# One operand of the next unit prepared ahead of another in a hand-written list of side work (attention, router and two feed-forward layers on one core)

## The chip, the cores and the metric

The kernel runs on one core of a Trainium2 chip. The metric is device time in microseconds: the median over several runs of one launch. Engines are named as in the profile: PE multiplies matrices (PEld loads its weights), DVE, ACT and POOL work elementwise, SP issues the transfers (DMA) between the chip's buffers and DRAM.

## The reference, cut to what matters

```python
x = attention(q, k, v)                       # windowed, 2304 tokens x 512
logits = x @ w_gate;  P = exp(logits - logits.max())
for _ in range(8):                           # the router's normalisation
    P /= P.sum(1, keepdims=True) + 1e-09
    P /= P.sum(0, keepdims=True) + 1e-09
    P *= N / E
out = 0
for e in range(8):                           # D = 512, F = 1024
    out += P[:, e:e + 1] * (np.maximum(x @ w1[e], 0.0) @ w2[e])
h = out @ w_in;  return (h * np.cos(h)) @ w_out      # F = 2048
```

## The kernel before

All products are in float32 written as sums of a high part and a low remainder: an operand x is kept as hi = x rounded (ACT writes it) and lo = x - hi (DVE or POOL writes it), and a product is hi*hi, hi*lo and lo*hi.

After the attention, the experts' layer runs over three blocks of 768 tokens, and inside a block over 32 *units* of 256 columns of F (4 units for each of 8 experts; `UPE` is 4, `NU1` is 32). A unit n is seven products of its first weight matrix with sums of quarters of x (a seven-product scheme), called by number in the order 5, 1, 4 of the unit before, 2, 3, 6, then the *batch*, then 7. The batch multiplies the hidden values of unit n-1 with its second weight matrix, in 6 tiles of 128 tokens (tt = 0 to 5), each into one of three banks `gT` in turn, which DVE then adds to the accumulator (the eviction, L1181 or, once the router's weights are in, L1191).

In the first block, ("moe", 0), the weights are not yet in the form the products need. It is made as side work, unit by unit, by generators: each `yield` ends a step, and the steps are called at fixed places among the products. The four that matter here:

- `prep_s(u)`: POOL makes four sums of quarters of the first matrix of unit u, tile `s` (L133).
- `prep_a(u)`: three ACT copies (hi, L143) and three DVE subtractions (lo, L146; the last one, of 128x1024, from `s`) fill `waX`, the first operand of unit u; then SP stores it to DRAM (`wd`, 1792 KB, L148) and loads the raw first matrix of unit u+2 (`ra`, two transfers, L105). Eight steps.
- `prep_b(u)`: ACT (hi, L160) and POOL (lo, L162) fill `wbX`, the second weight matrix of unit u; three stores of it (`wdp`, 256 KB each, L167). Six steps.
- `prep_sb(u)`: POOL makes four sums of quarters of the second matrix (L182), ACT their hi (L185), DVE their lo (L189), all in one tile `sb` that every unit uses in turn; SP stores hi and lo (`wdp`, 1024 KB, L192) and loads the raw second matrix of unit u+2 (`rb`, L105). These rows are used by later blocks only.

`prep_a`, `prep_b` and `prep_s` stand in the list `pre`, of which only the first entry is stepped; `prep_sb` stands in the list `sbq`. `slot()` steps `pre`, then `sbq`, then (by way of `feed`) `bg`, which holds the router's normalisation: a step A (three small DVE instructions, L410 to L412) and, three steps on, a step B (a matmul with `ones` on PE, L420, and three DVE instructions). There is a slot after products 5, 1, 4, 2 and 7 and after tiles 1 to 5 of the batch, and after each of those tiles `pre` is stepped once more. At the end of a unit the rest of `pre` is run down.

In unit n, `pre` begins with `prep_b(n)`, two steps of which run in the slots after products 5 and 1. Then, at product 4, `begin(n + 1)` adds `prep_a(n + 1)` and `prep_s(n + 2)`.

In units 2 to 4 `prep_sb(n)` has ten steps, one for each slot: ACT's L185 in the slot after product 4, DVE's L189 after tile 1 of the batch, the store and the load of `rb` after tile 3. From unit 5 on it has fewer steps, and L185 falls in the slot after product 5.

Every engine, SP among them, takes its instructions strictly in the order of the program; the framework puts in the waits for data and for buffers.

Of the kernel before, what the change touches and what calls it, by code (L numbers as in the profile page):

```python
# [29 lines left out]
def tile_attention_moe_cos_ffn(ctx, tc, q, k, v, w_gate, w1, w2, w_in, w_out, out):  # L30
# [8 lines left out]
    UPE = F // FU  # L39
# [33 lines left out]
    with tc.manual_schedule():  # L73
# [16 lines left out]
        def load_raw(u, ab):  # L90
            if u >= NU1 + NU2 or (u, ab) in raw_t:
                return
            t = rawp.tile([P, KC, FU] if ab == "a" else [P, 2, DM], F32, tag=f"r{ab}", name=f"r{ab}{u}")
            raw_t[u, ab] = t
            if u >= NU1:
                for c in range(2):
                    nc.sync.dma_start(out=t.rearrange("p k f -> p (k f)")[:, c * 512:(c + 1) * 512],
                                      in_=w32[4 * (u - NU1) + (0 if ab == "a" else 2) + c])
                return
            e, s = divmod(u, UPE)  # L100
            src = (w1[e][:, s * FU:(s + 1) * FU].rearrange("(k p) f -> p k f", p=P) if ab == "a"
                   else w2[e][s * FU:(s + 1) * FU, :].rearrange("(k p) d -> p k d", p=P))
            m = t.shape[1] // 2
            for c in range(2):
                nc.sync.dma_start(out=t[:, c * m:(c + 1) * m, :], in_=src[:, c * m:(c + 1) * m, :])  # L105
# [3 lines left out]
        def wa_of(u):  # L109
            return waX[:, u % 2].rearrange("p (o h k f) -> p o h k f", o=7, h=2, k=2)  # L110
# [15 lines left out]
        def prep_s(u):  # L126
            ra = raw_t[u, "a"]
            s4 = s_t[u] = rawp.tile([P, 4, 2, P], F32, tag="s4", bufs=1, name=f"s4_{u}")
            a11, a12 = ra[:, 0:2, :P], ra[:, 2:4, :P]
            a21, a22 = ra[:, 0:2, P:], ra[:, 2:4, P:]  # L130
            for o, x, y, op in ((0, a21, a22, ALU.add), (1, s4[:, 0], a11, ALU.subtract),
                                (2, a11, a21, ALU.subtract), (3, a12, s4[:, 1], ALU.subtract)):
                nc.gpsimd.tensor_tensor(out=s4[:, o], in0=x, in1=y, op=op)  # L133
                yield

        def prep_a(u):
            ra, s4 = raw_t[u, "a"], s_t[u]
            wa = wa_of(u)
            both = ra[:, :, :P].rearrange("p (o k) f -> p o k f", k=2)
            parts = [(wa[:, 0:2, 0], wa[:, 0:2, 1], both), (wa[:, 2, 0], wa[:, 2, 1], ra[:, 2:4, P:]),  # L140
                     (wa[:, 3:7, 0], wa[:, 3:7, 1], s4)]
            for hi, lo, x in parts:
                nc.scalar.activation(out=hi, in_=x, func=AF.Copy)  # L143
                yield
            for hi, lo, x in parts:
                nc.vector.tensor_tensor(out=lo, in0=x, in1=hi.bitcast(F32), op=ALU.subtract)  # L146
                yield
            nc.sync.dma_start(out=wd1[u], in_=waX[:, u % 2].bitcast(F32))  # L148
            if u + 2 < NU1:
                load_raw(u + 2, "a")  # L150
            yield
# [715 lines left out]
        bg, bg2, pre, feed, sbq = [], [], [], [], []  # L867
# [361 lines left out]
        def begin(n):  # L1229
            if n < len(steps):  # L1230
                kind, b, u = steps[n]
                if kind == "moe" and not b and u >= 2:
                    pre.append(prep_a(u))
            if n + 1 < len(steps):
                kind, b, u = steps[n + 1]
                if not b and kind == "moe" and u >= 3:
                    pre.append(prep_s(u))
# [52 lines left out]
        for n, s in enumerate(steps):  # L1290
            kind, b, u = s
# [20 lines left out]
            for m in (5, 1, 4, 2, 3, 6, 0, 7):  # L1312
# [12 lines left out]
                if m == 4:  # L1325
                    if n:
                        product(steps[n - 1], 4)
                    begin(n + 1)
                else:
                    product(s, m)  # L1330
# [75 lines left out]
```

## Time and profile before

| what | us |
|---|---|
| median of 3 runs | 1981.72 (1981.71 to 1982.1) |
| the profiled execution, whole | 1982.96 |
| its span (first to last instruction) | 1981.2 |
| PE busy | 1957.6 |
| DVE busy | 1555.7 |
| ACT busy | 862.6 |
| POOL busy | 964.7 |

The busy times are sums over the whole span, and the span is some 1.8 us shorter than the execution. Times in a trace count from the start of the span. Unit 2 of the first block begins at about 182 us, unit 3 at 198.6, unit 4 at 216.2 and unit 5 at 233.6.

### The profile page before, as it was taken

To read this page: it belongs to the slowest core of one execution; us is meant where nothing else is said; L and a number is where in the kernel's file an instruction comes from. 1 tells how busy PE (TensorE), PEld (TensorE's weight loads), DVE (VectorE), ACT (ScalarE), POOL (GpSimd) and SP (SyncE) were. 2 spreads that over 40 slices of the span, in tenths; PEclk is the share of its full clock that TensorE was granted. 3 is DMA by queue.
4 is the path that set the end of the run, shared out by engine and by line. 5 is a ranking of instruction groups with operands and counts; after the bars stand their busy time and mean duration, and the time that the engine had idled before them with its cause. 6 is when DMAs were issued, how large, how long until landed. Compare 5 with 4: busy or idle time off the path is not lost.

```text
span 1981.2 us, 31148 instructions
## 1 busy us (share of the span) xinstructions
PE 1957.6 (99%) x10977; PEld 1823.6 (92%) x10977; DVE 1555.7 (79%) x2655; ACT 862.6 (44%) x1617; POOL 964.7 (49%) x940
## 2 busy tenths in 40 slices
PE   8999999999999999999999999999999999999999
PEld 6668899999999999999999999999999999998898
DVE  7885777777777788988888877888877776757766
ACT  6885444444444333333333433333233354554543
POOL 5673566666666445454536622545454423333221
PEclk9999999999999999999999999999999999999999
DMA  7854888888888999998999888999998765554552
GB/s 194 221 141 146 294 294 312 302 310 311 295 309 302 321 333 314 339 336 320 340 326 326 277 285 280 328 337 334 330 306 297 242 223 195 197 218 175 207 192 96
DMA packets 293755, 540.05 MB, mean 273 GB/s; under 512 B 80256, under 2 KB 141792, under 8 KB 286432
## 3 DMA queue, kind: packets, MB, share of 16 engines
q1 hardware_dynamic: 292240, 537.74, 78.7%
q8 instruction: 87, 1.43, 0.3%
q14 instruction: 68, 0.56, 0.1%
q10 hardware_dynamic: 1360, 0.33, 0.1%
HBM read 384.32 MB, written 153.67 MB: 272 GB/s over the span
## 4 chain that ended last, share of the span: by engine, by line
PE 94%; DVE 2%; DMA 2%; ACT 1%; issue 1%; SPq 0%; POOL 0%; DVEq 0%; POOLq 0%; ACTq 0%
PE gT L1111 23%; PE y_moe L972 19%; PE z_moe L972 10%; PE gT L1201 7%; PE gT L1202 7%; PE gT L1200 7%; PE y_ffn L972 5%; PE x_moe L972 5%; PE z_ffn L972 2%; PE xbank L639 2%; DMA wbX<-wdp 1%; PE x_ffn L972 1%; PE s L537 1%; PE pt L603 1%; PE pt L601 1%
## 5 line engine op out<-in xcount | busy, mean ns | idle before, releaser
L1111 PE MATMUL gT<-hX,wbX 128*128 128x384 f32 x2688 | 538.7, 335 | 2.8 <-DMA wbX<-wdp 2.7
L1111 PEld LDWEIGHTS gT<-hX,wbX 128*128 128x128 f32 x2688 | 471.6, 188 | 5.5 <-DMA wbX<-wdp 2.1
L972 PE MATMUL y_moe<-xtT_moe,waX 128*128 128x384 f32 x1728 | 347.3, 335 | 0.0
L972 PEld LDWEIGHTS y_moe<-xtT_moe,waX 128*128 128x128 f32 x1728 | 304.4, 188 | 3.3 <-ACT s_moe L1001 0.6
L1123 DVE TENSOR_TENSOR acc_moe<-gT,acc_moe 128x384 f32<-128x384 f32 x432 | 237.7, 550 | 77.9 <-PE gT L1111 76.0
L1202 PE MATMUL gT<-wbX,hX 128*128 128x512 f32 x660 | 258.2, 391 | 0.0
L1201 PE MATMUL gT<-wbX,hX 128*128 128x512 f32 x660 | 258.1, 391 | 0.0
L1200 PE MATMUL gT<-wbX,hX 128*128 128x512 f32 x660 | 258.0, 391 | 0.0
L1001 ACT ACTIVATE s_moe<-y_moe 128x384 f32<-128x384 f32 x192 | 93.3, 486 | 350.5 <-PE y_moe L972 350.2
L1145 POOL TENSOR_TENSOR hodd<-hodd 128x384 f32<-128x384 f32 x128 | 156.0, 1238 | 139.2 <-DVE hX L1131 71.3
L1145 POOL TENSOR_TENSOR cX<-cX 128x384 f32<-128x384 f32 x128 | 145.7, 1158 | 157.3 <-DVE hX L1131 97.1
L961 POOL TENSOR_TENSOR hX<-cX,hX 128x768 fp32r<-128x768 f32 x44 | 83.5, 1913 | 249.3 <-ACT hX L958 208.6
L133 POOL TENSOR_TENSOR s<-ra 128x256 f32<-128x256 f32 x80 | 59.6, 745 | 236.5 <-DVE waX L146 164.0
L1191 DVE SCALAR_TENSOR_TENSOR acc_moe<-gT,prob,acc_moe 128x512 f32<-128x512 f32 x174 | 129.6, 747 | 37.5 <-PE gT L1202 35.7
L1202 PEld LDWEIGHTS gT<-wbX,hX 128*128 128x128 f32 x660 | 123.9, 188 | 25.9
L1200 PEld LDWEIGHTS gT<-wbX,hX 128*128 128x128 f32 x660 | 124.1, 188 | 25.5 <-DVE acc_moe L1191 0.7
L1201 PEld LDWEIGHTS gT<-wbX,hX 128*128 128x128 f32 x660 | 124.0, 188 | 24.3
L917 ACT ACTIVATE hX<-cX 128x768 fp32r<-128x768 f32 x64 | 43.9, 687 | 216.1 <-DVE cX L1004 216.1
L1131 DVE TENSOR_TENSOR hX<-cX,hX 128x768 fp32r<-128x768 f32 x112 | 131.4, 1173 | 1.6 <-ACT hX L1135 1.6
L1131 DVE TENSOR_TENSOR hX<-hodd,hX 128x768 fp32r<-128x768 f32 x112 | 127.4, 1137 | 0.9 <-ACT hX L1135 0.9
L972 PE MATMUL z_moe<-xtT_moe,waX 128*128 128x384 f32 x576 | 116.6, 336 | 2.6 <-DVE waX L146 2.6
L972 PE MATMUL z_moe<-xtB_moe,waX 128*128 128x384 f32 x576 | 116.1, 336 | 0.0
(211 smaller groups left out, 3768.3 us busy)
## 6 DMA issues: line engine op xcount, KB each, us to landing
waX<-wd SPq DMA_DIRECT2D x264, 512.0 KB, 5.5
wbX<-wdp SPq DMA_DIRECT2D x224, 512.0 KB, 6.6
wd<-waX SPq DMA_DIRECT2D x32, 1792.0 KB, 6.8
wdp<-sb SPq DMA_DIRECT2D x32, 1024.0 KB, 5.8
wdp<-wbX SPq DMA_DIRECT2D x96, 256.0 KB, 4.3
wbX<-wd SPq DMA_DIRECT2D x24, 1024.0 KB, 4.9
waX<-wd SPq DMA_DIRECT2D x88, 256.0 KB, 5.2
ra<-in_moe_w_dram SPq DMA_DIRECT2D x64, 256.0 KB, 7.3
```

The costliest lines, as they stand in the source:

```text
L133: nc.gpsimd.tensor_tensor(out=s4[:, o], in0=x, in1=y, op=op)
L961: eng.tensor_tensor(out=h[:, 1], in0=c, in1=h[:, 0].bitcast(F32), op=ALU.subtract)
L972: nc.tensor.matmul(ps[:, :HB], wa[:, WI[m], wl, kc, :], x[:, xl, kc, :], start=start and kc == 0 and n_ == 0, stop=stop and kc == 1 and n_ ...
L1001: nc.scalar.activation(out=t["s", i], in_=ps[:, :HB], func=AF.Copy)
L1111: nc.tensor.matmul(ps[:, :HB], w[:, u, wl, d * P:(d + 1) * P], x[:, xl, u, :], start=m in (1, 5, 2) and n_ == 0, stop=m in (4, 3, 2) and n ...
L1123: nc.vector.tensor_tensor(out=a, in0=ps[:, :HB], in1=a, op=ALU.add)
L1131: nc.vector.tensor_tensor(out=x[:, 1], in0=H[:, q], in1=x[:, 0].bitcast(F32), op=ALU.subtract)
L1145: nc.gpsimd.tensor_tensor(out=H[:, t[0], c], in0=H[:, t[1], c], in1=H[:, t[2], c], op=ALU.subtract)
L1191: nc.vector.scalar_tensor_tensor(out=a, in0=ps, scalar=pe, in1=a, op0=ALU.mult, op1=ALU.add)
L1200: nc.tensor.matmul(ps, hf[f][:, 0, ts], wb[:, f, 0, :], start=f == 0, stop=False)
L1201: nc.tensor.matmul(ps, hf[f][:, 0, ts], wb[:, f, 1, :], start=False, stop=False)
L1202: nc.tensor.matmul(ps, hf[f][:, 1, ts], wb[:, f, 0, :], start=False, stop=f == 1)
```

## The change

For units u of 2 to 5, `prep_a(u)` is put at the front of `pre` rather than at its end. `UPE + 1` is 5. For u = 2 `pre` is empty at that point, so the order differs for u = 3, 4 and 5, that is inside units 2, 3 and 4, in which two steps of `prep_b` have run already and four are left.

```diff
                 kind, b, u = steps[n]
                 if kind == "moe" and not b and u >= 2:
-                    pre.append(prep_a(u))
+                    pre.insert(0 if u <= UPE + 1 else len(pre), prep_a(u))
             if n + 1 < len(steps):
                 kind, b, u = steps[n + 1]
```

Where the steps fall in units 2, 3 and 4 (a1 to a3 are ACT's copies, a4 to a6 DVE's subtractions, a7 the store of `wd` and the load of `ra`; b3 is POOL's subtraction, b5 the three stores):

| place | before | after |
|---|---|---|
| after product 4 | b3 | a1 |
| after product 2 | b4 | a2 |
| after tile 1 | b5, b6 | a3, a4 |
| after tile 2 | a1, a2 | a5, a6 |
| after tile 3 | a3, a4 | a7, a8 |
| after tile 4 | a5, a6 | b3, b4 |
| after tile 5 | a7, a8 | b5, b6 |

b4, b6 and a8 issue nothing.

## Rows read from the trace of the kernel before

**Rows 1.** The page, busy time: engine, us, share of span, instructions.

```profile
PE 1957.6 (99%) x10977; PEld 1823.6 (92%) x10977; DVE 1555.7 (79%) x2655; ACT 862.6 (44%) x1617; POOL 964.7 (49%) x940
```

**Rows 2.** PE's waits, 195 to 260 us: who for whom, us, times, longest.

```profile
PE z_moe L972 <- DVE waX L146: 2.6, 3, 1.0
```

**Rows 3.** Timeline of PE: start, us, what [idle before <- releaser].

```profile
200.08 0.97 PE L972 MATMUL z_moe<-xtT_moe,waX 128*128 128x384 f32 x4 [1.00 <-DVE waX L146]
200.89 0.42 PE L420 MATMUL gT<-prob,ones 128*128 128x152 f32 x2
...
217.72 0.97 PE L972 MATMUL z_moe<-xtT_moe,waX 128*128 128x384 f32 x4 [1.00 <-DVE waX L146]
...
234.73 0.97 PE L972 MATMUL z_moe<-xtT_moe,waX 128*128 128x384 f32 x4 [0.64 <-DVE waX L146]
```

**Rows 4.** Timeline of DVE, in the batches of units 3 and 4.

```profile
208.81 0.68 DVE L1181 TENSOR_TENSOR acc_moe<-gT,acc_moe 128x512 f32<-128x512 f32 x1
...
212.01 1.28 DVE L1181 TENSOR_TENSOR acc_moe<-gT,acc_moe 128x512 f32<-128x512 f32 x2
...
214.03 0.68 DVE L146 TENSOR_TENSOR waX<-ra,waX 128x512 fp32r<-128x512 f32 x1
...
215.23 0.41 DVE L146 TENSOR_TENSOR waX<-ra,waX 128x256 fp32r<-128x256 f32 x1
...
216.45 1.22 DVE L146 TENSOR_TENSOR waX<-s,waX 128x1024 fp32r<-128x1024 f32 x1
217.59 0.68 DVE L1181 TENSOR_TENSOR acc_moe<-gT,acc_moe 128x512 f32<-128x512 f32 x1
...
230.22 1.41 DVE L1191 SCALAR_TENSOR_TENSOR acc_moe<-gT,prob,acc_moe 128x512 f32<-128x512 f32 x2
```

**Rows 5.** Timeline of SP in unit 3: issues of transfers.

```profile
212.15 0.36 SPq L192 DMA_DIRECT2D wdp<-sb  x1
...
217.70 0.33 SPq L148 DMA_DIRECT2D wd<-waX  x1
218.07 1.43 SPq L105 DMA_DIRECT2D ra<-in_moe_w_dram  x2
```

**Rows 6.** DMA issues: KB each, us to landing; then stores of `sb`, 150 to 260.

```profile
wd<-waX SPq DMA_DIRECT2D x1, 1792.0 KB, 6.7
...
ra<-in_moe_w_dram SPq DMA_DIRECT2D x1, 256.0 KB, 7.3
...
DMA to landing us min/median/max: 4.9/4.9/7.1
```

**Rows 7.** Timeline of ACT in units 3, 4 and 5.

```profile
205.38 1.06 ACT L185 ACTIVATE sb<-sb 128x1024 fp32r<-128x1024 f32 x1 [1.09 <-POOL sb L182]
206.92 0.49 ACT L1001 ACTIVATE s_moe<-y_moe 128x384 f32<-128x384 f32 x1 [0.49 <-PE y_moe L972]
...
223.08 1.06 ACT L185 ACTIVATE sb<-sb 128x1024 fp32r<-128x1024 f32 x1 [1.14 <-POOL sb L182]
...
236.97 1.07 ACT L185 ACTIVATE sb<-sb 128x1024 fp32r<-128x1024 f32 x1 [0.23 <-POOL sb L182]
```

**Rows 8.** Timeline of PE: tiles 3 and 5 of batches; product 6 of unit 5.

```profile
210.78 0.39 PE L1200 MATMUL gT<-wbX,hX 128*128 128x512 f32 x1
...
213.79 0.39 PE L1200 MATMUL gT<-wbX,hX 128*128 128x512 f32 x1
...
231.02 0.50 PE L1200 MATMUL gT<-wbX,hX 128*128 128x512 f32 x1
...
239.69 1.20 PE L972 MATMUL y_moe<-xtT_moe,waX 128*128 128x384 f32 x6
```

**Rows 9.** Stretches of PE: us, busy (instructions), granted clock, DMA share, GB/s.

```profile
18.00:20.00 2.00, 1.25 (x8) 0.80 0.99 308
20.00:22.00 2.00, 2.00 (x8) 0.50 1.11 323
22.00:24.00 2.00, 2.00 (x15) 0.85 1.12 345
```

## The prediction, made before the changed kernel was run

> **What bounds the kernel now.** I read the page first: PE is busy for nearly the whole span [rows 1], so a change outside PE pays only where it removes a wait of PE, and costs where it adds one. Next the list of PE's waits over the stretch that the change touches: there is one entry, product 5 (`z_moe`) waiting three times for the lo parts of `waX` [rows 2]. The timeline of PE places them at the starts of units 3, 4 and 5: 1.00, 1.00 and 0.64 us [rows 3]. Each is the first product that reads what `prep_a` made in the unit before. Then I followed the other engines through one unit, in the order in which the moved steps reach them: DVE, SP, the transfers, ACT. Units 2 and 3 repeat each other at a distance of 17.64 us (200.08 and 217.72 [rows 3]), so unit 3 serves for both.
>
> **What the change can give.** DVE's last subtraction a6 begins at 216.45 and lasts 1.22 [rows 4]: 217.67, and PE goes on at 217.72. After the change a4 to a6 stand around the eviction of tile 2, from 212.01 on. Consecutive DVE instructions overlap by 0.08 (216.45 + 1.22 against 217.59), so a4 0.68, one eviction 0.68, a5 0.41 and a6 1.22 less 3 x 0.08 end at 214.76: 2.9 us earlier, ahead of PE's need. All three waits go, 2.64 us; no more than that can be won.
>
> It isn't all won. DVE's work only changes order, and in the batches of units 2 and 3 it is nearly gapless. The normalisation's step A now comes behind a6, and ends where the last eviction began, 217.59 (+0.08); PE's matmul L420 needs it. In unit 2's place that is 200.03 against L420's start at 200.89 [rows 3]: 0.8 us won rather than 1.00. In unit 4 step A is absent, but the eviction of tile 2 has no room: it ends at 230.22 + 0.75 = 230.97 and tile 5, which takes the same bank, begins at 231.02 [rows 8]; a4 ahead of it delays tile 5 by 0.6, which nearly eats the 0.64. In unit 3 the same bank has room (213.79 against 213.29).
>
> **What it moves on SP.** a7 now stands in the slot after tile 3, and `slot()` steps `pre` before `sbq`: so the store of `wd` and both loads of `ra` come ahead of the store of `sb` on SP, where before the store of `sb` was issued at 212.15 and a7 at 217.70 [rows 5]. The store of `wd` must wait for a6 and SP takes its instructions in order. For t, the end of a6: `wd` is issued at t, the second `ra` at about t + 1.1, `sb` at t + 1.9 (0.33 and 1.43 of issuing with the gaps between).
>
> Landing: the second `ra` needs 7.3 us [rows 6], so t + 8.4. The `sb` store of 1024 KB behind it needs its bytes moved: `wd` with 768 KB more takes 6.7 against 4.9, 1.8 us, so 1024 KB take 2.4. I take t + 10.8. Bounds: if it need not queue, t + 1.9 + 4.9 = t + 6.8; if it only starts when `ra` has landed, t + 8.4 + 4.9 = t + 13.3. The longest landing of an `sb` store in this stretch is 7.1 rather than 4.9 [rows 6], with a store of `wd` and loads before it in the queue; a wait behind earlier bytes is thus real, and I stay near the queueing value.
>
> The Trainium skill, DMA: Bandwidth & Descriptors, section on the anatomy of one DMA, fits a transfer (of the other issuing path) as 2.0 us plus bytes over 436 GB/s. As an estimate by that page, `wd`, two `ra` and `sb` together, 3.4 MB, land in 9.8 us, and the sum below would be 3 us smaller; the rows' durations are a little longer than the fit (6.7 against 6.2 for `wd`), and I use the rows.
>
> **Who waits for it.** `sb` is a single tile. ACT's L185 of the next unit overwrites what the store reads, so it waits for the landing. Before, the store landed at 212.15 + 4.9 = 217.05 and L185 came at 223.08 [rows 7]: 6 us of room. Behind L185 on ACT stand a2 and the copy of product 6 (L1001); DVE's add, step A, all evictions and a4 to a6 follow that copy. So each late landing makes the next a6 late, and that the next landing: one chain through three units.
>
> Unit 2: a6 ends at 214.76 - 17.64 = 197.1; `sb` lands at 207.9.
> Unit 3: L185 at 207.9, not 205.38. It takes 1.06, a2 some 0.4 (under the 0.49 of a wider copy), so L1001 at 209.3, not 206.92: +2.4. The eviction of tile 0 ends at 208.81 + 0.68 + 2.4 = 211.9; tile 3, PE at 210.78, waits for it: +1.2. The eviction of tile 2 ends at 212.01 + 0.68 + 0.6 (a4) + 2.4 = 215.7; tile 5, at 213.79, comes at 215.75: +2.0. Step A ends at 217.67 + 2.4 = 220.1, and L420 (200.89 + 17.64 = 218.53) is at +1.6. a6 ends at 217.1.
> Unit 4: `sb` lands at 227.9; L185 at +4.8, the copy behind it at +5.0. The eviction of tile 2 ends at 230.97 + 5.0 + 0.6 = 236.6; tile 5 at +5.6; at product 5 the old wait of 0.64 is gone, so PE is at +5.0. a6 ends 1.5 after that eviction (0.41 + 1.22 less overlaps), 238.0.
> Unit 5: `sb` lands at 248.8. Here L185 stands already behind product 5, before at 236.97, so it is 11.8 us late. Behind it is the copy of product 1 (L1001): 248.8 + 1.07 + 0.49 less 0.1 of overlap = 250.26. PE's product 6 adds into the bank which that copy reads. Before it ran at 239.69; now at 250.3: **+10.6 us**, of which 5.6 are one empty stretch of PE (ready at 244.7). From there the old order holds, and nothing in it is late again: the next `sb` store has no `wd` ahead of it.
>
> **The clock.** The trace has one fall of PE's clock inside the run, at the end of a stretch in which PE had been waiting (busy 1.25 of 2.00 us): the granted clock is 0.80, 0.50 and 0.85 in three stretches of 2 us, that is at the lower of its levels, 1.2 instead of 2.4 GHz, for part of them [rows 9]. What it cost is 2 x (0.20 + 0.50 + 0.15) = 1.7 us of work. 5.6 us without work is emptier than what stood before this one. I take one such fall, +1.7; bounds 0 and two falls, 3.4.
>
> **What costs nothing.** b3 changes place in the program, but not among POOL's own instructions: between the last sum of one `prep_sb` and the first of the next POOL has nothing else. `wbX` is read a unit later. The loads of `rb` and the stores b5 land later, behind `sb`, by some 10 us; what they bring is read a unit or more on, so they are covered by a whole unit of PE (17.64 us). POOL's sums `s` can start 2.9 us earlier, which nobody waits for.
>
> **Sum.** +10.6 + 1.7 = +12.3, on the profiled execution's 1982.96: 1995.3. That execution is 1.24 above the median shown, so in the runs' scale 1994.0. A landing 1 us shorter or longer is worth three, since three stores stand in the chain.
>
> **The rivals.**
> (a) *The store of `sb` doesn't queue*: it lands at t + 6.8. Then L185 of unit 3 and 4 isn't late, PE is 1.6 ahead, a6 of unit 4 ends at 231.4 and `sb` lands at 238.2; L185 of unit 5 is still 1.25 late, and product 6 starts at 239.7, as before. Time 1981.8: no change. For it: 16 engines share the transfers, and 4.9 is the usual landing. Against: 7.1 when something is ahead. A landing of about 8.6 is where the loss reaches 4 us (10.6 less 3 x 2.2).
> (b) *L185 never waits* (the store's reads are over long before its landing counts, or its bytes overtake): only the gains stay, 1.9 to 2.6 us, 1979.1 to 1979.8, faster but within 0.2%. It decides if L185 in unit 5 still starts by 237. Against it: the tile is single, and the store reads just what L185 writes.
> (c) *Partial queueing*, bytes of both stores interleaved, landing about t + 9: +5.2, perhaps a fall of the clock: 1987 to 1989.
> (d) *Longer landing*, t + 12 to 13.3, with two falls of the clock: +14 + 3.4 to +18 + 3.4: 1999 to 2003.
>
> **Chances.** Forecast 0.62 (1990 to 1998); (a) 0.10; (b) 0.07; (c) 0.12; (d) 0.09. A measurement of this kernel can tell about 0.2%, 4 us, from no change. Forecast, (c) and (d) hold 0.83, of which 0.01 falls short of those 4 us: slower 0.82. (a) and (b) hold 0.17 and stay within 0.2%, since the three waits are 2.64 us in all; I take 0.02 of it for a gain that I haven't seen: faster 0.02, same 0.15 + 0.01 = 0.16. The range holds the forecast and (c) and the lower end of (d): 1986 to 1999.
>
> **What the changed profile would show.** Right: the wait of `z_moe` on `waX` gone; on SP L192 right behind L148 and L105 in units 2 to 4; L185 waiting for the DMA `wdp<-sb` some 4, 5 and more us; PE waiting for evictions in two batches and, longest of all, in unit 5 for ACT's copy `s_moe`; perhaps 0.50 of clock near 250. Wrong: landings of `sb` near 5 us, or L185 at its old places; then (a) or (b) holds. A PE wait for `waX` that stays would mean that the steps are not where I put them.

## The result and the profile after

| | before | after |
|---|---|---|
| median, us (6 runs of each on one chip) | 1983.11 (1981.71 to 1985.42) | 1997.03 (1996.43 to 1998.85) |
| ratio, 95% interval | 1 | 1.0073 [1.0062, 1.0083] |
| span of the profiled execution | 1981.2 | 1995.2 |
| PE busy | 1957.6 | 1963.2 |

The changed kernel is 13.9 us slower; the spans differ by 14.0. Line numbers are the same in both. Up to unit 2 the new trace runs 0.27 us ahead (product 7 of unit 1, the last ahead of unit 2, starts at 180.87, before at 181.14), so 0.27 is added wherever a start of after is compared with one of before. The starts of the other kernels are put on the scale of before by the same product.

First the list of PE's waits over the whole span of the kernel after (who for whom, us, times, longest), cut to the lines that are new and one that shrank:

```profile
PE y_moe L972 <- ACT s_moe L1001: 7.7, 1, 7.7
...
PE gT L1200 <- DVE acc_moe L1191: 2.6, 1, 2.6
PE gT L1200 <- DVE acc_moe L1181: 2.5, 1, 2.5
...
PE gT L1111 <- DMA wbX<-wdp: 1.3, 2, 1.0
...
PE gT L420 <- DVE prob L412: 0.3, 1, 0.3
```

The wait for `waX` [rows 2] is gone, as the change intends. In its place stand 13.1 us of others. The last of them, 0.3 us, is that of L420 for step A, which now comes behind a6. The other 12.8 follow from one wait that PE never shows, ACT's, in the timeline of ACT of the kernel after (start, us, what, idle before and its releaser):

```profile
208.56 1.06 ACT L185 ACTIVATE sb<-sb 128x1024 fp32r<-128x1024 f32 x1 [4.57 <-DMA wdp<-sb]
...
228.51 1.06 ACT L185 ACTIVATE sb<-sb 128x1024 fp32r<-128x1024 f32 x1 [3.73 <-DMA wdp<-sb]
...
251.38 1.06 ACT L185 ACTIVATE sb<-sb 128x1024 fp32r<-128x1024 f32 x1 [9.48 <-DMA wdp<-sb]
252.34 0.47 ACT L1001 ACTIVATE s_moe<-y_moe 128x384 f32<-128x384 f32 x1
```

Before, L185 waited for POOL's sums, 0.2 to 1.1 us [rows 7]; now it waits for the store out of the single tile `sb`. The timeline of SP of the kernel after shows why the store is late:

```profile
196.87 0.34 SPq L148 DMA_DIRECT2D wd<-waX  x1
197.31 1.39 SPq L105 DMA_DIRECT2D ra<-in_moe_w_dram  x2
198.75 1.29 SPq L192 DMA_DIRECT2D wdp<-sb  x1
200.15 3.40 SPq L105 DMA_DIRECT2D rb<-in_moe_w_dram  x2
...
217.67 0.33 SPq L148 DMA_DIRECT2D wd<-waX  x1
...
219.54 1.31 SPq L192 DMA_DIRECT2D wdp<-sb  x1
...
238.57 0.33 SPq L148 DMA_DIRECT2D wd<-waX  x1
...
240.44 1.30 SPq L192 DMA_DIRECT2D wdp<-sb  x1
```

In unit 3 the store of `sb` had gone out 5.6 us ahead of that of `wd` [rows 5]; now it goes out 1.9 us behind it. L185 starts the moment it has landed, so the landing counted from the issue of `wd` is 208.56 - 196.87 = 11.7, 228.51 - 217.67 = 10.8 and 251.38 - 238.57 = 12.8 us. From its own issue a store of `sb` now takes up to 10.8, before at most 7.1 [rows 6]; here the view of the tile `sb`, 180 to 275 us, after:

```profile
DMA to landing us min/median/max: 4.0/8.9/10.8
```

The timeline of PE of the kernel after, at the marks that answer to [rows 3] and [rows 8]:

```profile
199.81 0.53 PE L420 MATMUL gT<-prob,ones 128*128 128x152 f32 x2 [0.30 <-DVE prob L412]
...
212.43 0.79 PE L1200 MATMUL gT<-wbX,hX 128*128 128x512 f32 x1 [2.49 <-DVE acc_moe L1181]
...
220.61 0.53 PE L420 MATMUL gT<-prob,ones 128*128 128x152 f32 x2
...
233.17 0.79 PE L1200 MATMUL gT<-wbX,hX 128*128 128x512 f32 x1 [2.58 <-DVE acc_moe L1191]
...
252.86 2.29 PE L972 MATMUL y_moe<-xtT_moe,waX 128*128 128x384 f32 x6 [7.70 <-ACT s_moe L1001]
...
263.91 1.23 PE L972 MATMUL y_moe<-xtT_moe,waX 128*128 128x384 f32 x6
```

The loss grows along the chain. L420 in unit 2's place is 0.8 us early (199.81 + 0.27 against 200.89), a unit later 2.4 late (220.61 + 0.27 against 218.53), product 6 of unit 5 is 13.4 late (252.86 + 0.27 against 239.69). Product 7, the last of unit 5, is 15.2 late (263.91 + 0.27), by this row of before:

```profile
248.94 1.23 PE L972 MATMUL y_moe<-xtT_moe,waX 128*128 128x384 f32 x6
```

The end of the span is 14.3 late on the same scale: about 1 us comes back later, where the wait of L1111 for `wbX` is 1.3 instead of 2.7.

The clock, in stretches of 2 us of PE of the kernel after (columns as in [rows 9]):

```profile
212.00:214.00 2.00, 1.57 (x4) 0.54 0.04 8
214.00:216.00 2.00, 2.00 (x8) 0.60 0.00 0
...
232.00:234.00 2.00, 0.83 (x2) 0.66 0.00 0
234.00:236.00 2.00, 2.00 (x6) 0.50 0.00 0
236.00:238.00 2.00, 2.00 (x10) 0.98 0.00 0
250.00:252.00 2.00, 0.00 (x0) 0.50 1.09 381
252.00:254.00 2.00, 1.14 (x4) 0.50 0.20 68
254.00:256.00 2.00, 2.00 (x7) 0.50 0.74 287
256.00:258.00 2.00, 2.00 (x9) 0.86 0.96 273
```

After each of the three long waits PE works at the lower level, 1.2 GHz, for some 3 to 4 us. What that costs is read from the time up to the same later product, without the wait. From tile 3 to product 7 it takes 5.94 us behind the first wait (212.43 to 218.37) and 5.56 behind the second (233.17 to 238.73), before 4.37 (210.78 to 215.15) and 4.34 (228.17 to 232.51). From product 6 to product 7 of unit 5 it takes 11.05 (252.86 to 263.91), before 9.25 (239.69 to 248.94). That is 1.6, 1.2 and 1.8, together 4.6 of the 5.6 us by which PE's busy time grew.

### The profile page after: what moved, and what is told of

Its sections match the earlier page's. It is cut to its first block, busy times and chain, and to the rows that moved or that the text cites. A ratio compares the mean times of both kernels' runs of the same rounds, so it can differ in the third digit from the quotient of the medians.

```text
span 1995.2 us, 31146 instructions
## 1 busy us (share of the span) xinstructions
PE 1963.2 (98%) x10977; PEld 1827.0 (92%) x10977; DVE 1555.5 (78%) x2655; ACT 861.9 (43%) x1617; POOL 965.2 (48%) x940
## 4 chain that ended last, share of the span: by engine, by line
PE 92%; DMA 3%; DVE 2%; ACT 1%; issue 1%; SPq 0%; POOL 0%; ACTq 0%; POOLq 0%; DVEq 0%
PE gT L1111 23%; PE y_moe L972 19%; PE z_moe L972 9%; PE gT L1201 7%; PE gT L1200 7%; PE gT L1202 7%; PE y_ffn L972 5%; PE x_moe L972 5%; PE z_ffn L972 2%; PE xbank L639 2%; PE x_ffn L972 1%; PE s L537 1%; DMA wbX<-wdp 1%; DMA wdp<-sb 1%; DMA waX<-wd 1%
## 5 line engine op out<-in xcount | busy, mean ns | idle before, releaser
L1111 PE MATMUL gT<-hX,wbX 128*128 128x384 f32 x2688 | 538.3, 334 | 1.7 <-DMA wbX<-wdp 1.3
L1111 PEld LDWEIGHTS gT<-hX,wbX 128*128 128x128 f32 x2688 | 471.7, 188 | 4.6 <-DMA wbX<-wdp 1.8
```

The source lines that it names most:

```text
L1111: nc.tensor.matmul(ps[:, :HB], w[:, u, wl, d * P:(d + 1) * P], x[:, xl, u, :], start=m in (1, 5, 2) and n_ == 0, stop=m in (4, 3, 2) and n ...
```

## The experiments

Ratios are to the kernel before on the same chip, in runs of the same batch: 1983.26 us (median of 21) for the first four, 1982.37 (21) for the others. Where an edit shifts lines, the profile's numbers shift by some.

**1. The new order on ACT, DVE and POOL, the old order on SP.** The issues of `prep_a` are held until `prep_sb` has issued its own:

```diff
+def out_a():
     nc.sync.dma_start(out=wd1[u], in_=waX[:, u % 2].bitcast(F32))
     if u + 2 < NU1:
         load_raw(u + 2, "a")
+if 3 <= u <= UPE + 1:
+    held.append(out_a)
+else:
+    out_a()
...
 # prep_sb, behind its store and the load of rb
+while held:
+    held.pop(0)()
```

> The changed kernel, with one thing put back: on SP the store of sb and the loads of rb come again ahead of the store of wd and the loads of ra in units 2 to 4; the order on ACT, DVE and POOL stays as changed. Theory (a chain through the single tile sb: L185 waits for the landing of a store that stands behind wd and ra on SP): the wait of L185 on the DMA is gone (0 us), the three waits of PE for waX too, so the time is 1.9 to 2.6 us below the kernel before, some 16 us below the changed one. Rival 1 (the new order on DVE and ACT itself costs, since a4 to a6 stand ahead of evictions that PE waits for): at least some 5 us of the loss stay, PE still waits 2 us or more for evictions. Rival 2 (transfers crowded into the last third of the unit): they are as crowded as before, so most of the loss stays.

Measured: 1980.73 us (1979.57 to 1983.44), ratio 0.9986 [0.9977, 0.9995]. The list of PE's waits, 180 to 300 us, of this kernel has two lines:

```profile
PE gT L429 <- DVE prob L421: 0.6, 2, 0.3
PE gT L1209 <- DVE acc_moe L1200: 0.5, 1, 0.5
```

and its ACT (L192 is L185 of the others) never waits for the DMA in units 3 to 5:

```profile
204.23 1.07 ACT L192 ACTIVATE sb<-sb 128x1024 fp32r<-128x1024 f32 x1
...
234.99 1.05 ACT L192 ACTIVATE sb<-sb 128x1024 fp32r<-128x1024 f32 x1
```

So the whole loss lies in the order of issues on SP, and the rest of the change is a small gain: 2.5 us, by the interval 1.0 to 4.6. Of it 1.5 us are PE's waits in this stretch (2.64 before, 1.1 now); in the trace product 7 of unit 5 comes 1.7 us earlier than before (247.30 less 0.10, against 248.94). What lies beyond that is within the interval. This version is the fastest of the three, by 0.05 to 0.23% of the kernel before.

**2. The same SP order, but the store reads another tile.** In units 2 to 4 the store of `sb` has its place, size and target, and reads `waX`:

```diff
+if 2 <= u <= UPE:
+    other = waX[:, (u + 1) % 2, :8 * FU].bitcast(F32).rearrange("p (o h f) -> p o h f", o=4, h=2)
+    nc.sync.dma_start(out=pair_rows(u)[:, 1:5], in_=other)
+else:
     nc.sync.dma_start(out=pair_rows(u)[:, 1:5], in_=hl.bitcast(F32))
```

> The changed kernel; in units 2 to 4 the store of sb has the same place, size and target, but reads from waX instead of sb, so that L185 has nothing to wait for (the second-weight sums of units 2 to 4 that later blocks read are thereby left out). Theory: as if the store landed at once for L185: no wait of L185 on the DMA, 1.9 to 2.6 us below the kernel before, though the store still lands 9 to 11 us after its issue. Rival 1 (order on DVE and ACT): PE still waits 2 us or more for evictions in units 3 and 4. Rival 2 (crowded transfers slow what reads them): the time stays within 4 us of the changed kernel.

Measured: 1982.29 us (1978.61 to 1983.78), ratio 0.9989 [0.998, 0.9998]. Its SP issues in the order of the changed kernel:

```profile
197.85 0.34 SPq L148 DMA_DIRECT2D wd<-waX  x1
198.29 1.39 SPq L105 DMA_DIRECT2D ra<-in_moe_w_dram  x2
199.73 1.29 SPq L194 DMA_DIRECT2D wdp<-waX  x1
201.13 3.42 SPq L105 DMA_DIRECT2D rb<-in_moe_w_dram  x2
```

The transfers queue as in the changed kernel: the store lands 9.7 us after its issue (median of the three, 8.9 to 10.9; in the changed kernel 9.7, 8.9 and 10.8), by the list of its DMA issues:

```profile
wdp<-waX SPq DMA_DIRECT2D x3, 1024.0 KB, 9.7
```

L185 doesn't wait for the DMA, and PE has the same 1.1 us of waits as in experiment 1. Hence the late transfers cost nothing by themselves (late loads of `rb`, a full queue); the cost is that `sb` is overwritten by L185 while a late store reads it.

**3. The old order of the work, the new order on SP.** Here the store of `sb` and the loads of `rb` are held until `prep_a` has issued its own, in the kernel before:

```diff
+if 2 <= u <= UPE:
+    held.append(out_sb)
+else:
+    out_sb()
...
 # prep_a, behind its store and the load of ra
+while held:
+    held.pop(0)()
```

> The kernel before, with one thing changed: in units 2 to 4 the store of sb and the loads of rb are issued on SP right behind the store of wd and the loads of ra, which stand at their old, late place; ACT, DVE and POOL keep the old order. Theory: the chain closes from a later start. With a landing 11.7 us after wd's issue (what the changed kernel showed), a6 of unit 2 at 200.0 gives L185 of unit 3 at 211.7 instead of 205.4 (+6.3), unit 4 about +12, unit 5 about +21; product 6 of unit 5 at about +20, one to three falls of the clock: 20 to 24 us above the kernel before, so more than the changed kernel. Rival 1 (the order on DVE and ACT is what costs): within 2 us of the kernel before.

Measured: 2006.03 us (2004.78 to 2006.33), ratio 1.011 [1.0097, 1.0124], +22.8. The waits of ACT, 180 to 275 us, and of PE:

```profile
ACT sb L188 <- DMA wdp<-sb: 24.2, 3, 10.3
```

```profile
PE y_moe L981 <- ACT s_moe L1010: 8.6, 1, 8.6
PE gT L1209 <- DVE acc_moe L1200: 4.5, 1, 4.5
PE gT L1209 <- DVE acc_moe L1190: 4.1, 1, 4.1
PE z_moe L981 <- DVE waX L147: 1.5, 2, 1.0
```

The order on SP alone does the harm, and more of it, since `wd` still leaves late: on the scale of before its stores in units 2 to 4 go out at 200.06, 223.19 and 246.13, in the changed kernel at 197.14, 217.94 and 238.84. The two halves of the change don't add (-2.5 and +22.8 against +13.9): the earlier a4 to a6 start each link earlier, by 2.9, 5.3 and 7.3 us.

**4. Only the loads of `ra` behind `sb`.** SP's order is then `wd`, `sb`, `rb`, `ra`:

```diff
 nc.sync.dma_start(out=wd1[u], in_=waX[:, u % 2].bitcast(F32))
-if u + 2 < NU1:
+if 3 <= u <= UPE + 1:
+    held.append(lambda: load_raw(u + 2, "a"))
+elif u + 2 < NU1:
     load_raw(u + 2, "a")
...
 # prep_sb, behind its store and the load of rb
+while held:
+    held.pop(0)()
```

> The changed kernel, but in units 2 to 4 only the two loads of ra (512 KB) are moved behind the store of sb; the store of wd (1792 KB) still stands ahead of it. Theory: the landing of sb after wd's issue falls from 10.8 to 12.8 us to about 9.5 to 10.5, and three such landings stand in the chain: 5 to 7 us less than the changed kernel, 7 to 9 us above the kernel before. Rival 2 (crowding, whatever the order): no more than 2 us less than the changed kernel. If it were only the wait of SP for a6 that holds the store of sb, not the bytes ahead of it: 1.5 us per landing less, and the landing from sb's own issue stays at 9 to 11 us.

Measured: 1991.34 us (1989.5 to 1993.41), ratio 1.0038 [1.0024, 1.0052], +8.1. ACT and SP of this kernel:

```profile
207.33 1.06 ACT L188 ACTIVATE sb<-sb 128x1024 fp32r<-128x1024 f32 x1 [2.53 <-DMA wdp<-sb]
```

```profile
197.69 0.34 SPq L149 DMA_DIRECT2D wd<-waX  x1
198.07 0.43 SPq L195 DMA_DIRECT2D wdp<-sb  x1
```

The store lands 207.33 - 197.69 = 9.6 us after the issue of `wd`, instead of 11.7; the three are 9.6, 9.6 and 10.3. So moving the two loads of `ra`, 512 KB, is worth 1.2 to 2.5 us of landing, and the 1792 KB of `wd` ahead are the larger part: with them alone in front the store takes 9.1 us from its own issue (median), not 4.9 [rows 6]. An earlier landing, a shorter chain: 5.8 us are won back for some 1.9 us of landing on the average, a slope of three, as the prediction has it (product 6 of unit 5 is 7.7 us late instead of 13.4). Why the landing is earlier isn't settled by this run alone. The store is also issued 1.5 us earlier behind `wd` (0.38 us instead of 1.88), and its landing from its own issue, 9.1 to 9.8, stays in the 9 to 11 that the other reading named beforehand. For the bytes speaks what the DMA engines had moved from the issue of `wd` to the landing: 3.1, 3.1 and 3.3 MB at 324 to 327 GB/s here, 3.9, 3.7 and 4.4 MB at 336 to 344 in the changed kernel.

**5 to 7. One unit at a time.** The steps are moved in one unit alone, the last, the first or the middle one of the three:

```diff
-pre.append(prep_a(u))
+pre.insert(0 if u == UPE + 1 else len(pre), prep_a(u))   # e4
+pre.insert(0 if u == 3 else len(pre), prep_a(u))         # e5
+pre.insert(0 if u == 4 else len(pre), prep_a(u))         # e6
```

> The new order for u = 5 alone, that is inside unit 4; units 2 and 3 as before. Theory: one link of the chain, the last. a6 of unit 4 ends at 233.05, sb lands 11 to 13 us later, L185 of unit 5 (236.97 before) waits till 244 to 246, PE's product 6 comes at 245.5 to 247.5 instead of 239.69: +6 to +8, one fall of the clock +1.7: 7 to 10 us above the kernel before. Rival 1 (order on DVE and ACT): at most +0.6 from tile 5, the same as before.

> The new order for u = 3 alone, inside unit 2. Theory: the first link alone. sb lands at 197.1 + 11.7 = 208.8, L185 of unit 3 is 3.4 us late, the copy behind it 2.9, DVE's batch 2.9; a6 of unit 3 is again the last that product 5 waits for, at +2.9. Unit 3 has the old order on SP, so the chain ends: +2.9, and 0 to 1 of a fall of the clock: 2.5 to 4 us above the kernel before. Rival (links are independent of each other): a third of the whole, 4.7 us.

> The new order for u = 4 alone, inside unit 3. Theory: a6 of unit 3 ends at 214.8, sb lands 10.8 to 11.7 us later, at 225.6 to 226.5; L185 of unit 4 (223.08 before) is 2.5 to 3.4 us late, the copy behind it and DVE's batch 2.3 to 3.2, and product 5 of unit 5 waits for that a6: +2 to +3, 0 to 1 of clock: 2 to 4 us above the kernel before. The three single links (units 2, 3 and 4) should add to some 14 us, what the whole change costs. Rival (links are independent of each other): 4.7 us each.

| moved in | median us | ratio | over before | L185 waits |
|---|---|---|---|---|
| unit 4 | 1992.66 | 1.0052 [1.0038, 1.0066] | +10.3 | 10.1 |
| unit 2 | 1985.90 | 1.0018 [1.0009, 1.0027] | +3.5 | 5.1 |
| unit 3 | 1985.42 | 1.0014 [1.0005, 1.0023] | +3.1 | 4.3 |

Each link alone makes one wait of L185, and each shows one fall of the clock behind it. The wait in unit 5 costs most. There L185 stands right ahead of the copy that frees the bank of product 6, as the rows of ACT above show (251.38, 252.34): this link alone, without a chain, costs +10.3 (7.5 to 13.1 by the interval; 7 to 10 was expected). The chain shows in the starts of L185 in units 3, 4 and 5. On the scale of before each link alone makes it 3.5, 2.6 and 9.6 us late, the whole change 3.5, 5.7 and 14.7. At product 6 the last link alone makes 8.3 of the 13.4 us; the 5.1 that the chain brings are near the 5.0 at which the prediction had PE there. The three medians add to 16.9, 3 us over the whole change, which intervals of 2 to 3 us on either side don't tell from 13.9.

**8. PE kept busy in the longest wait.** In the changed kernel PE makes 66 transposes of the identity into a bank that nobody reads, ahead of product 6 of unit 5:

```diff
+if m == 6 and s == ("moe", 0, 5):
+    for _ in range(66):
+        nc.tensor.transpose(gT[3][:, :P], ident, ident)
```

> The changed kernel with 66 transposes of the identity into an idle bank ahead of product 6 of unit 5, about 7.3 us of work that nothing reads, where PE stood 7.7 us waiting for ACT's copy. Theory on the clock: the fall to 0.50 near 250 comes from that empty stretch; with PE busy in it the clock stays at 1.00 there, product 6 takes 1.2 rather than 2.3 us, and the time is 1.7 us below the changed kernel (0 to 2.5, depending on whether the transposes outlast the wait). The waits of L185 on the DMA stay. Rival: the clock falls there anyway, and the time is the same or longer.

Measured: 1994.89 us (1994.15 to 1995.89), ratio 1.0063 [1.0049, 1.0076]; +12.5 against +13.9 of the changed kernel. PE in this kernel:

```profile
246.39 7.37 PE L1326 MATMUL gT<-ident 128*128 128x128 f32 x66
253.51 1.30 PE L972 MATMUL y_moe<-xtT_moe,waX 128*128 128x384 f32 x6
```

```profile
250.00:252.00 2.00, 2.00 (x21) 1.00 1.05 388
252.00:254.00 2.00, 2.00 (x20) 1.00 0.89 314
254.00:256.00 2.00, 2.00 (x11) 1.00 0.51 197
```

L185 waits as before (8.8 us, from 9.5), but the clock stays at the upper level and product 6 takes 1.30 instead of 2.29. From product 6 to product 7 of unit 5 PE takes 9.36 us (253.51 to 262.87), in the changed kernel 11.05. The third fall is thus worth about 1.7 us, and it comes from PE's standing still. The medians show 1.4. A second tile for `sb`, which would take the wait away at its root, wasn't tried.

## Why the prediction was right

Forecast were +12.3 us on the profiled execution and a median of 1994.0 within 1986 to 1999; measured +14.0 and 1997.0. Of the 3.0 us between the medians 1.4 lie in the kernel before, which came out at 1983.11 in six runs where the forecast started from 1981.72 in three. By its own steps:

- **What is won.** Right. a6 begins at 195.63 + 0.27 for a forecast end of 197.1 (measured 195.90 + 1.22 = 197.12); all waits for `waX` went; L420 came 0.8 us early, as worked out. Experiment 1 measures the whole gain: 2.5 us, for 2.64 at the most.
- **The order on SP.** Right: `wd`, two `ra`, `sb`, in 1.9 us. Experiments 1 and 3 show that it alone makes the loss.
- **Who waits.** Right: L185, for the single tile. Experiment 2 removes just this tie and the loss is gone. The waits of L185 rule out rival (b), the landings (a) and (c).
- **The landing.** The mechanism is right, the term too small: t + 10.8 was forecast for each of the three, and 11.7, 10.8 and 12.8 came. By the Trainium skill, DMA: Bandwidth & Descriptors, section on the anatomy of one DMA, the estimate was 9.8 for this burst; no landing of this kernel was that short, so the rows were nearer. I had counted the bytes ahead alone, at the 437 GB/s that 768 KB in 1.8 us make. Behind `sb` on the queue stand two loads of `rb` and more, whose bytes move in the same time. From the issue of `wd` to the landing the DMA engines moved 3.9, 3.7 and 4.4 MB, at 336 to 344 GB/s; `wd`, `ra` and `sb` have 3.4. So the three landings differ by the bytes of later transfers, 0.5, 0.3 and 1.0 MB, that got through first. What these cost the store wasn't tested, and why more got through before the third stays open; it was as long in experiment 2 (12.8), without a chain.
- **The chain.** Its size follows these landings. The first was 0.9 late against the forecast, and L420 in unit 4 stood at +2.4 instead of +1.6. The store of `wd` in unit 4 went out at 238.84 on the scale of before, where 238.0 was forecast; with the third landing 2.0 longer L185 came 2.8 later than forecast, and product 6 at +13.4 instead of +10.6.
- **The clock.** One fall at 1.7 us was taken, two were the upper bound; three came. The first cost nothing: DVE is busy without a gap from 210.33 to the end of step A, and L420 follows that end at once:

```profile
219.58 0.32 DVE L410 TENSOR_REDUCE gT<-prob 128x18 f32<-128x162 f32 x1
219.94 0.28 DVE L411 RECIPROCAL gT<-gT 128x18 f32<-128x18 f32 x1
220.25 0.30 DVE L412 TENSOR_TENSOR prob<-prob,gT 128x144 f32<-128x144 f32 x1
```

  A PE at full clock would have waited for the same step (220.25 + 0.30 against L420 at 220.61). The second hid for the most part behind the eviction that frees the bank of tile 5: it ends at 236.30 + 0.75 = 237.05, and the tile starts at 237.37, so some 0.3 show. Only the third stood free, 1.8, and experiment 8 gives 1.7 of it back. So the number of falls was wrong, and the sum is nearly right by luck: nothing in the prediction said that two more would be hidden.
- **Given back later.** About 1 us in the waits for `wbX` after 300 us, which wasn't forecast. These loads differ in each of the kernels run here (2.7 before, 0.4 to 2.3 in the others), and no experiment was made on them.

The sum in new figures: +13.4 at product 6, +1.8 for the clock there, less 1.0 later: 14.2, against 14.0 to 14.3 by the ends of the spans.

## What to carry to other kernels

When a step of side work is moved, list what it issues on each queue in the new order, and ask of every transfer now behind it which tile it reads and who next writes that tile; a single buffer turns a late store into a wait of the engine that fills it. Move the arithmetic and leave the order of the issues: here the same move was worth -2.5 us instead of +13.9. A wait that repeats in each unit is priced along the chain, but the link with the least slack must be priced by itself, since it alone can cost most of the loss. Here it is the last: before, the store of unit 4 landed at 235.4 and L185 came at 236.97, 1.6 us of room instead of 6.

## What was not expected of the hardware

A store of 1024 KB, 4.9 us when nothing is ahead of it [rows 6], took 8.9 to 10.8 from its issue behind 1792 KB and two loads of 256 KB, and 9.1 to 9.8 behind the 1792 KB alone. Waits of PE of 2.5 and 2.6 us, not only the one of 7.7, were each followed by 3 to 4 us of work at the lower clock; where PE was given work in the longest one, the clock stayed at 1.00. The length of a wait alone doesn't tell: with the steps moved in unit 2 alone, PE waited 2.2 us up to 212.72 and the clock stayed at 1.00; it fell only behind the next wait, 1.9 us up to 220.90.
